# Sliding-window attention mixed with a long convolution: the spectrum's products reordered, lag 0 as a full tile, and a new order of all tasks

## The chip, the cores and the metric

The kernel runs on one core of a Trainium2 chip. Its time is the device time of one execution in microseconds (us); of several executions the median is given. The core has five queues of instructions that run beside each other: PE (matrix products; the weight loads of PE are shown apart as PEld), DVE and ACT (vector and scalar work), POOL, and SP, which here only starts transfers. Transfers (DMA) are started from the queues of SP, POOL and ACT and share 16 engines. Each queue runs its instructions strictly in the order in which they are given.

## What is computed

Two layers see the same input `x` (2048 positions, 640 channels) and are mixed by a gate per position. The first is an attention over 8 positions at distance 2, with 32 heads of 20 channels. The second is a state-space layer: a kernel `K` of 2048 lags for each channel is built from 192 complex modes, and the input is convolved with it by Fourier transforms.

```python
# attention
qkv = (x @ wqkv)                       # 32 heads of 20; keys and values at pos - 2*w, w = 0..7
o = softmax(q . k * scale) . v
a = o @ wo
# state-space layer
P = exp(logdA[:, :, None] * l)         # l = position, rounded to the input's type (bf16)
K = einsum("dn,dnl,dn->dl", Cc, P, dB).real
y = irfft(rfft(u, 2L) * rfft(K, 2L))[:L] + u * Dskip
# mix
g = sigmoid((x * gate_w).sum(-1))
out = g * a + (1 - g) * y
```

Since the position is rounded to bf16, many lags share one value: `K` takes only as many different values as there are rounded positions, and its spectrum is a product of those values with a constant matrix.

## The kernel before

The work is cut into some 1400 named tasks. Each task is a small piece of code for one engine: one group of matmuls, one eviction from PSUM, one transfer. The tasks' numbers stand in a list, `SEQ` (line 50), that was written out ahead of time; a letter behind a number picks the engine where there is a choice (A for ACT, D for DVE, S for SP, G for POOL). `Plan.emit` (line 132) issues the tasks in this order, so the list fixes the order of every queue. What a task needs, and which buffers it takes and gives back, decides only when it waits.

The stages, by the names of their tasks:

- `ld…` load the inputs; `turn` transposes `x` on PE and `late` makes queries, keys and values (L277), 60 groups of five products.
- The parameters of the modes are worked out on DVE and ACT and stored as bf16 pieces (`sp`). `kred` and `kmix` (L622 to L626) sum the modes for lag 0 and add `Dskip`.
- Attention goes in eight cores of 256 positions: `prod` (DVE, L335), `lg` (PE, L341), `max`, `exp`, `at`, then the values `vc` are loaded (L329), weighed by `pv` (DVE, L404), gathered on PE by `gat` (L410) and projected by `wo` (L428). The result goes to memory as `gaS`.
- The kernel's values are made in ten chunks: `arg` (PE, L758) makes the arguments, `act` (ACT, L770 and L772) takes sine and exponential, `pq` (DVE, L789 to L791) multiplies, `kmm` (PE, L807) sums over the modes, and `fin` (DVE, L865) stores 20 groups of 32 lags for every channel in `E`.
- The spectrum of the kernel has two parts, part 0 of six chunks (192 columns) and part 1 of four (128 columns). `move` puts the 640 lags of each part on 128 rows in `M5` = 5 tiles (`KE`). Then for each of 16 steps (8 blocks of four frequencies, real and imaginary part) a tile `W` of constants is loaded from memory (`wl`, L900, ring of three buffers) and `ks` (L912) multiplies it. Real parts have one more product at the end: lag 0, the same for all frequencies, from the single row `KD` against a row of ones (L916). `ske` evicts.
- The input's transform: `rows` load `x` in another layout (L993), `fu` (PE, L1027) and `fp` (PE, L1062) transform, `ta`, `tc`, `Y` (DVE, L1089 to L1095) multiply by the kernel's spectrum. `inv` (L1120) and `yp` (L1162) transform back; `psi` and `gaf` (L1136, L1142) load constants and the gated attention, and the result is scaled, added and stored (`tt`, `mx`, `st`, `out`).

Lag 0's value travels a way of its own: `kds` (L847) stores it, `kdl` (L851) loads it as one row, and `kdp` (L855) puts it in order on POOL.

Of the kernel before, what the change touches and what calls it, by code (L numbers as in the profile page):

```python
# [20 lines left out]
S = 2048  # L21
# [3 lines left out]
W = 8  # L25
# [25 lines left out]
13S 12S 24 18A 16S 23 35 36A 37A 20G 14S 15S 0G 4G 21 32 25 28 29 39 3S 22D 38 41 27 26 30 10S 8G 9S 100 11S 7S 108 5G 103G 17S 6S 2S 110 42 252S 109A 111A 31 104 105A  # L51
112 106 40 107A 43 44 113D 52 53 45 125 156 54 126D 157D 82 49 46 47 48 50 60D 61D 145 135 146A 136A 120 118 63 119A 149 133 114 150A 134A 55 115A 143 141 144A 142A 121D
62 57 51 68 69 70 77D 65 78 79 116 177 129 122 130A 83 178A 131 132A 71 185 186A 58 183 184A 147 66 148A 162 181 19G 1157G 56 72 101 1G 102G 1146G 163A 88A 182A 179 117A
180A 158 139 73 86 87 89 74 159A 137 140A 90A 138A 153 127 123A 76 85 93 128A 124 59 67 64 75 187S 84 91D 92 95 80 154A 260 97 98 262 94 96 81 99 550 253 261 160 166 161A
263 170 167A 171A 254 264 266 265 268 255 151 209 267 269 152A 256 211 257 210A 212A 270 271 272 296 33 298 34 176 155G 551 258S 552 164 554 217 553 555 556 273 274 558
557 559 560 561 562 564 563 565 297 566 299 165D 300 302 218D 568 567 569 570 571 572 573 547G 301 574 575 576 304 168 169D 578 577 579 174 175D 580 582 581 583 213 584
586 215 585 597 587 830 835 840 596 598 599 600 601 602 603 604 605 275 295S 259S 548G 588 214D 590 589 216D 276 277 606 591 607 608 592 610 303 198 609 612 278 611 613
614 616 615 617 593 618 620 619 621 594 622 305 624 623 625 279D 332 280 306 199A 172 626 628 281 283 173D 334 634 549 595 282D 643 636 627 629 630 632 631 633 642 644
645 646 647 648 649 307 1155S 650 652 651 653 219G 688 654 655 656 657 658 659 660 284 662 661 664 663 665 635 666 668 667 200 639 670 637 638 640 669 671 672 674 201D
285D 206 308 673 675 207A 680 309 676 677 641 310 689 286 678 287D 682 681 679 690 691 692 694 693 333 335 695 696 697 288 698 290 700 289A 699 701 336 338 337 702 683  # L60
703 704 705 684 188 706 707 339 685 340 291D 708 686 709 710 711 712 713 714 716 715 717 718 719 720 721 722 723 292 331G 311 312 734 735 687 726 313 728 724 727 736 189A
725 737 293A 241 738 740 341 342 243 739 741 242A 742 743 744 745 343 746 747 245 244D 316 246D 748 194 344 729 345 749 368 346 247 750 752 751 369 754 753 248D 756 195A
755 757 202 780 781 203A 370 372 731 371 758 760 759 761 196 762 208 249 294 347 348 373 764 374 376 197A 763 765 314 250A 766 730 768 375 377 317 767 769 315A 770 771
732 782 318A 783 319 220 378 251S 910 911 349 221A 784 320 786 379 785 787 321D 322 323A 733 772 774 788 380 324 326 789 325A 327A 381 773 790 792 791 793 204 777 404 794
775 776 796 190 191D 795 797 798 799 800 802 801 803 778 382 804 328 205A 806 805 807 329A 230 808 810 350 231A 809 811 405 812 813 814 815 816 817 912 913 351A 192 914
916 234 406 352 355 193A 915 917 918 919 235A 353 920 407 922 354A 921 923 238 924 818 820 779 408 409 410 412 239A 926 356 819 925 928 927 929 821 357A 403G 367G 383 956
384 957 330 930 411 932 931 933 413 823 414 934 936 822 935 937 358 360 938 415 940 359A 361A 939 416 226 227A 941 942 362 364 944 417 363A 365A 943 945 440 385 388 442
824 386 418 825 391 946 958 236 947 959 387A 960 441 443 962 389 237A 961 963 826 392 828 390A 827A 393A 829A 444 445 228 229A 446 448 948 447 224 964 966 449 232 225A
965 967 968 394 233A 450 419 366 1003 420 950 451 395A 396 970 452 969 397A 222 972 398 453 949 951 971 973 223A 952 974 976 400 975 399A 977 978 401A 439S 1002 240 1147S
1148S 1149S 1150G 1151G 1152S 1153S 1154G 402 421 424 454 455 476 422 979 980 982 423A 981 983 425 984 986 985 987 477 988 989 426A 831 478 479 990 992 833 832A 991 993  # L70
1004 834A 1005 953 427 954 1006 428 1008 1007 429A 1009 836 1010 430 837A 994 955 480 1012 1011 1013 431A 838 1014 995 1016 1015 839A 1017 432 1018 433A 1019 481 434 1020
# [611 lines left out]
class KGen:  # L683
# [51 lines left out]
    def plan(self, pl, pa, pk, hold, params, opened, fin):  # L735
# [4 lines left out]
        for c in range(NCH):  # L740
# [41 lines left out]
            for u in range(3):  # L782
# [543 lines left out]
```

## Time and profile before

| | |
|---|---|
| median of three runs | 404.74 us (402.11 to 405.25) |
| the profiled execution | 401.13 us, of which 399.3 us are the span of its instructions |
| mean granted clock of PE | 0.935 of full speed |
| busy | PE 333.3, DVE 300.0, ACT 302.3, POOL 50.9 us |
| moved by DMA | 49.86 MB, 125 GB/s over the span |

The profile gives for each instruction its engine, line, output and inputs, start and duration. Matmuls are pipelined: their durations overlap, so the pace of a block is read from the starts. In a timeline a row is a start, a duration, the engine and line, output and inputs, and how many instructions were merged; brackets hold the idle time of the engine before it and what ended that. "Issue" in brackets means that the engine waited for nothing that the profile shows. In a row of groups the two numbers behind the bar are the busy time in us and the mean of one in ns. A view of windows gives the busy time of each engine in stretches of the span.

### The profile page before, as it was taken

To read this page: it belongs to the slowest core of one execution; us is meant where nothing else is said; L and a number is where in the kernel's file an instruction comes from. 1 tells how busy PE (TensorE), PEld (TensorE's weight loads), DVE (VectorE), ACT (ScalarE), POOL (GpSimd) and SP (SyncE) were. 2 spreads that over 40 slices of the span, in tenths; PEclk is the share of its full clock that TensorE was granted. 3 is DMA by queue.
4 is the path that set the end of the run, shared out by engine and by line. 5 is a ranking of instruction groups with operands and counts; after the bars stand their busy time and mean duration, and the time that the engine had idled before them with its cause. 6 is when DMAs were issued, how large, how long until landed. Compare 5 with 4: busy or idle time off the path is not lost. (4 is left out here: it accounts for less than half of the span.)

```text
span 399.3 us, 14980 instructions
## 1 busy us (share of the span) xinstructions
PE 333.3 (83%) x6664; PEld 209.5 (52%) x6686; DVE 300.0 (75%) x420; ACT 302.3 (76%) x456; POOL 50.9 (13%) x82
## 2 busy tenths in 40 slices
PE   0499997968897999899957999999899994799860
PEld 0355452333354446445432656668777793688750
DVE  4979996686898989889894486869689752347782
ACT  3989986786999899989955888877587652365782
POOL 8710011200300010120201000000000231000022
PEclk9989998599899999999985999999999997699996
DMA  8971557851313127160599724461032859744027
GB/s 278 380 182 32 170 149 197 150 142 23 78 16 76 48 64 144 31 144 3 129 187 173 155 76 107 93 203 30 16 103 77 286 138 222 165 125 135 3 70 197
DMA packets 55761, 49.86 MB, mean 125 GB/s; under 512 B 33534, under 2 KB 46752, under 8 KB 55696
## 3 DMA queue, kind: packets, MB, share of 16 engines
q1 hardware_dynamic: 50896, 34.93, 36.0%
q0 software_dynamic: 4080, 13.64, 13.1%
q8 instruction: 52, 0.85, 0.9%
q10 hardware_dynamic: 720, 0.33, 0.3%
q14 instruction: 13, 0.11, 0.1%
HBM read 37.00 MB, written 11.89 MB: 122 GB/s over the span
## 5 line engine op out<-in xcount | busy, mean ns | idle before, releaser
L770 ACT ACTIVATE big<-ar 128x576 bf16<-128x576 int16 x120 | 72.5, 654 | 20.2 <-PE ar L758 18.6
L277 PE MATMUL tb<-bufA 128*128 128x512 bf16 x278 | 75.4, 400 | 6.1 <-DMA bufA<-in_A_wqkv_dram 2.6
L912 PE MATMUL tb<-KE,W 128*64 128x192 bf16 (+1 forms) x1280 | 62.3, 242 | 8.8 <-DMA W<-c_spec 8.6
L758 PE MATMUL ar<-Rarg,L 64*128 64x288 bf16 (+1 forms) x480 | 55.3, 283 | 12.7 <-ACT big L770 10.2
L912 PEld LDWEIGHTS <-W 128*64 128x64 bf16 x1280 | 47.5, 114 | 15.9 <-DMA W<-c_spec 9.3
L772 ACT ACTIVATE big<-ar 128x832 bf16<-128x832 f32 x60 | 49.8, 869 | 4.7 <-PE ar L758 3.7
L277 PEld LDWEIGHTS <-bufA 128*128 128x128 bf16 x300 | 32.7, 122 | 35.9 <-issue 12.6
L404 DVE TENSOR_TENSOR pv<-vc,asb 128x4096 bf16<-128x4096 bf16 (+1 forms) x24 | 46.0, 1931 | 6.2 <-PE tb L410 6.1
L758 PEld LDWEIGHTS <-L 64*128 64x128 bf16 x480 | 19.0, 95 | 52.3 <-issue 48.8
L457 ACT ACTIVATE bufA<-tb 128x384 bf16<-128x384 f32 (+1 forms) x36 | 18.9, 528 | 20.6 <-PE tb L912 11.7
L807 PE MATMUL kps<-tbx 128*32 128x20 bf16 (+1 forms) x2560 | 25.9, 175 | 9.7 <-issue 9.7
L807 PEld LDWEIGHTS <-tbx 128*32 128x32 bf16 (+1 forms) x2560 | 22.4, 92 | 15.2 <-issue 12.9
L457 ACT ACTIVATE tbx<-ar 128x512 bf16<-128x512 f32 (+1 forms) x31 | 20.4, 699 | 11.6 <-PE ar L1062 7.5
L1089 DVE TENSOR_TENSOR tbx<-tbx,bufA 128x768 bf16<-128x768 bf16 (+1 forms) x32 | 14.5, 487 | 19.1 <-ACT bufA L457 14.0
L335 DVE TENSOR_TENSOR prod<-qk 128x2048 bf16<-128x2048 bf16 x20 | 24.1, 1220 | 4.1 <-PE lg L341 2.2
L428 PE MATMUL tb<-wo_sb,oT 128*128 128x320 bf16 x160 | 26.9, 306 | 0.0
L335 DVE TENSOR_TENSOR prod<-uga 128x2048 bf16<-128x2048 bf16 x20 | 24.1, 1220 | 3.3 <-PE lg L341 3.1
L791 DVE TENSOR_TENSOR tbx<-big 128x1280 bf16<-128x1280 bf16 x30 | 24.6, 818 | 0.0
L457 ACT ACTIVATE big<-ar 128x1024 bf16<-128x1024 f32 x19 | 18.7, 1023 | 7.3 <-PE ar L1027 7.1
L410 PE MATMUL tb<-pv,ind 128*64 128x512 bf16 (+1 forms) x192 | 23.1, 365 | 0.0
L789 DVE TENSOR_TENSOR tbx<-big 128x1024 bf16<-128x1024 bf16 x30 | 20.5, 685 | 1.0 <-ACT big L770 0.5
L790 DVE TENSOR_TENSOR tbx<-big 128x1024 bf16<-128x1024 bf16 x30 | 20.5, 685 | 0.0
(168 smaller groups left out, 527.7 us busy)
## 6 DMA issues: line engine op xcount, KB each, us to landing
W<-c_spec SPq DMA_DIRECT2D x32, 320.0 KB, 3.2
Sprm<-pc SPq DMA_DIRECT2D x12, 240.0 KB, 2.9
L<-Sprm SPq DMA_DIRECT2D x80, 36.0 KB, 3.1
vc<-vS SPq DMA_DIRECT2D x8, 327.5 KB, 6.7
vc<-vS POOLq DMA_DIRECT2D x8, 327.5 KB, 5.7
gaS<-ga SPq DMA_DIRECT2D x8, 320.0 KB, 2.8
uga<-gaS POOLq DMA_DIRECT2D x8, 320.0 KB, 10.9
asb<-aS SPq DMA_DIRECT2D x16, 128.0 KB, 2.8
```

What stands on the lines that cost most here:

```text
L277: nc.tensor.matmul(ppf, self.wq[:, kt, which * D + e:(which + 1) * D:5], self.xT[:, c0 // 1024, kt, c0 % 1024:c0 % 1024 + SC], start=(kt = ...
L335: nc.vector.tensor_tensor(b[e][:], self.part(ch, 0)[:, e, o:o + C].unsqueeze(1).to_broadcast([128, W, C]), win(self.part(ch, 1)[:, e, :], ...
L404: nc.vector.tensor_tensor(b["pv", e][:, 0:2 * n], taps, aw, ALU.mult)
L410: nc.tensor.matmul(b["op", e][64 * a:64 * a + 64, 0:n, :], self.twin, b["pv", e][:, a:2 * n:2, w, :], start=(w == 0), stop=(w == HV - 1), ...
L428: nc.tensor.matmul(apf[:, :320], b["oT"][:, e, i * 128:(i + 1) * 128], wo_sb[:, e, hf * 320:(hf + 1) * 320], start=(e == 0), stop=(e == 4))
L457: nc.scalar.activation(o, i, ACT.Identity)
L758: nc.tensor.matmul(ar[:, g2, a0:a0 + ncol], L[rows, sb, gp, l0:l0 + 128], R[rows, c0:c0 + ncol], start=True, stop=True, tile_position=(64 ...
L770: nc.scalar.activation(dst[:, 2 * gp:2 * gp + 2, sub, :], ar[:].bitcast(I16)[:, :, 0:2 * SW:2], ACT.Sin, scale=SCL)
L772: nc.scalar.activation(dst[:, 2 * gp:2 * gp + 2].rearrange("p g s n -> p g (s n)"), ar[:, :, 0:2 * EW], ACT.Exp)
L791: nc.vector.tensor_tensor(qq[:, :, :, :], trg[:, :, KI:].rearrange("p a (v m) -> p a v m", v=2), exq[:, :, KI:].unsqueeze(2).to_broadcast( ...
L807: nc.tensor.matmul(kps[32 * g:32 * g + 32, h, NM * ql:NM * ql + NM], pt[rows, k, v, :], qq[rows, k, v, :], start=(g not in started), stop= ...
L912: nc.tensor.matmul(kp[64 * c:64 * c + 64, fl], w["t"][:, nf * h + fl, m, :], self.KE[p][:, m, c].rearrange("p x g -> p (x g)"), start=(m = ...
```

## The change

Four edits.

1. In `kmm`, `ks` and `yp` the loops are turned: the index over which is summed goes outside, and the outputs go inside, so that products that add to the same place are no longer neighbours. The `start` flag is now set once for each PSUM bank, at the first product that writes it.
2. Lag 0 becomes a sixth tile of 128 rows: `KD` has 128 rows, zero but for the first, `one` likewise, and its products come first (`m = -1`) in the same loop as the five others.
3. A new task `kdz` on POOL zeroes `KD` before the values are put in.
4. `SEQ` is another list: all tasks in a new order, with other engines for 83 of them.

```diff
@@ KGen.plan, kmm
-                    for ql in range(4 * j, 4 * j + 4) if u == 1 else range(8):
-                        for v in range(2):
+                    for v in range(2):
+                        for ql in range(4 * j, 4 * j + 4) if u == 1 else range(8):
...
@@ KSpec
-        self.one = keep.tile([1, 64], BF16, name="one")
-        self.nc.gpsimd.memset(self.one[:], 1.0)
+        self.one = keep.tile([128, 64], BF16, name="one")
+        self.nc.gpsimd.memset(self.one[:], 0.0)
+        self.nc.gpsimd.memset(self.one[0:1], 1.0)
...
-        self.KD = kk.tile([1, 2, 80, 4], BF16, name="KD")
+        self.KD = kk.tile([128, 2, 80, 4], BF16, name="KD")
...
-        t = pl.add("kdl", "SG", load, deps=[t], after=self.past)
-        self.kd = pl.add("kdp", "G", lambda _: nc.gpsimd.tensor_copy(self.KD[:].rearrange(...), ...), deps=[t])
+        t = pl.add("kdl", "SG", load, deps=[t] + self.past)
+        z = pl.add("kdz", "G", lambda _: (opened(), nc.gpsimd.memset(self.KD[:], 0.0)), deps=self.past)
+        self.kd = pl.add("kdp", "G", lambda _: nc.gpsimd.tensor_copy(self.KD[0:1].rearrange(...), ...), deps=[t, z])
...
@@ KSpec.part, spec
-                    for fl in range(nf):
-                        for m in range(M5):
+                    first = -1 if ro == 0 else 0
+                    for m in range(first, M5):
+                        for fl in range(nf):
                             for c in range(2):
-                                nc.tensor.matmul(kp[64 * c:64 * c + 64, fl], w["t"][:, nf * h + fl, m, :], self.KE[p][:, m, c]...,
-                                                 start=(m == 0), stop=(m == M5 - 1 and ro == 1), ..., tile_position=(0, 64 * c))
-                        if ro == 0:
-                            for c in range(2):
-                                nc.tensor.matmul(kp[64 * c:64 * c + 64, fl], self.one[:], self.KD[:, c, 8 * c0:8 * c1]...,
-                                                 start=False, stop=True, ..., tile_position=(0, 64 * c))
+                                wt = self.one[:] if m < 0 else w["t"][:, nf * h + fl, m, :]
+                                ke = self.KD[:, c, 8 * c0:8 * c1] if m < 0 else self.KE[p][:, m, c]
+                                nc.tensor.matmul(kp[64 * c:64 * c + 64, fl], wt, ke.rearrange("p x g -> p (x g)"),
+                                                 start=(m == first and fl == 0), stop=(m == M5 - 1), ..., tile_position=(0, 64 * c))
...
@@ Conv.tail, fin
-                for k, v in enumerate(vs):
-                    for ro in range(2):
+                for ro in range(2):
+                    for k, v in enumerate(vs):
...
-                                                 start=(ro == 0), stop=(ro == 1), ...)
+                                                 start=(ro == 0 and k == 0), stop=(ro == 1), ...)
```

The new list in the places that the prediction reads. On DVE, `kred` and `kmix` now come before the products of core 0 (before: between those of core 1). On PE the end of part 0 of the spectrum reads

```
before  ... ks0,12 fp06 ks0,13 fu15 ks0,13 ks0,14 fp07 ks0,14 ks0,15 fu16 fu17 ks0,15 fu18 fu19 ks1,0 ks1,1 fp10 ks1,2 ...
after   ... ks0,9 fp05 fu17 ks0,9 fu18 fu19 ks0,10 (2) move (2) ks0,11 (2) fp06 (2) ks0,12 (2) fp07 ks0,13 (2) ks0,14 (2) ks0,15 (2) ks1,0 fp07 fp10 ks1,1 ...
```

On POOL the queue reads `rows0` to `rows7`, then the values of cores 5 and 6, `phi1`, the values of core 7, `psi`, `gaf`; before, five of the rows and the values of cores 5 and 7 were SP's. At the start the first two loads of `x` and one of the weights have moved to ACT's queue.

More of the change, by code (lines that the diff above doesn't have):

```diff
@@ L900, in load @@
                 queue(nc, e).dma_start(w["t"][:].rearrange("p f m x -> p (f m x)"), self.w_d[k])
-            ld = self.ld = pl.add(f"wl{p}{k}", "S", load, after=[getattr(self, "ld", None)] + self.past, acq=["W"])
+            ld = self.ld = pl.add(f"wl{p}{k}", "S", load, deps=self.past, after=[getattr(self, "ld", None)], acq=["W"])
             for h in range(4 // nf):
@@ L1162, in fin @@
                                 nc.tensor.matmul(yp[64 * j:64 * j + 64, h, 160 * k:160 * k + 160], psi[64 * h:64 * h + 64, 32 * j + v, ro, :], C[64 * h:64 * h + 64, 64 * ro + 32 * j + v, :],
-                                                 start=(ro == 0), stop=(ro == 1), skip_group_check=True, tile_position=(64 * h, 64 * j))
+                                                 start=(ro == 0 and k == 0), stop=(ro == 1), skip_group_check=True, tile_position=(64 * h, 64 * j))
             def scale(_, n=n, vs=vs):
```

82 lines of the change are left out of this document (40 added, 42 removed).

## The prediction

> **What bounds the kernel now.** I read the totals first, then the busy time by stage, because an average over 399 us hides which engine sets which stretch.
>
> ```profile
> span 399.3 us, 14980 instructions
> PE 333.3 (83%) x6664; PEld 209.5 (52%) x6686; DVE 300.0 (75%) x420; ACT 302.3 (76%) x456; POOL 50.9 (13%) x82
> ```
>
> ```profile
> 68.00:205.00 137.00, 122.83 (x2523) 60.45 (x2538) 116.97 (x146) 122.72 (x189) 14.70 (x22) 0.94 0.41 87
> 205.00:212.00 7.00, 0.52 (x54) 0.41 (x43) 5.63 (x8) 0.23 (x1) 0.00 (x0) 0.69 1.30 179
> 212.00:220.00 8.00, 7.68 (x63) 2.83 (x51) 3.17 (x4) 5.69 (x11) 1.43 (x2) 0.63 1.06 175
> 220.00:330.00 110.00, 107.92 (x2442) 79.67 (x2438) 81.98 (x121) 83.86 (x129) 7.25 (x12) 1.00 0.43 117
> 330.00:350.00 20.00, 12.28 (x244) 10.38 (x242) 6.67 (x17) 6.38 (x12) 0.66 (x2) 0.68 0.90 198
> 350.00:376.00 26.00, 24.39 (x660) 20.25 (x657) 16.85 (x39) 16.28 (x23) 0.00 (x0) 0.98 0.32 93
> ```
>
> The columns are window, length, then busy time of PE, weight loads, DVE, ACT, POOL, the granted clock, the DMA share and GB/s. From 68 to 205 us three engines share the work: PE 90%, ACT 90%, DVE 85% busy, and PE is without work for 14.2 us. From 220 to 330 us PE is busy 98% while DVE and ACT are at 75 and 76%: this stretch, and again 350 to 376 us (94%), is set by PE alone. Two holes interrupt it, 205 to 212 and 330 to 350 us; in both the DMA share is high (1.30, 0.90) and the clock falls (0.69 and 0.63 around the first, 0.68 in the second). All of the spectrum's products (L912, L916) lie after 219.6 us, that is, where PE is the bound.
>
> **Lag 0, the largest term.** The real half of each frequency block ends with a product of one row; the imaginary half has none. The PE timeline shows both, first with 192 columns (part 0), then with 128 (part 1):
>
> ```profile
> 219.60 0.60 PE L912 MATMUL tb<-KE,W 128*64 128x192 bf16 x10
> 220.13 0.27 PE L916 MATMUL tb<-KD,one 1*64 1x192 bf16 x2
> ...
> 221.07 0.40 PE L341 MATMUL lg<-prod,ind 128*32 128x512 bf16 x4
> ```
>
> ```profile
> 227.22 1.02 PE L912 MATMUL tb<-KE,W 128*64 128x192 bf16 x20
> 228.17 0.30 PE L758 MATMUL ar<-Rarg,L 64*128 64x288 bf16 x2
> ```
>
> ```profile
> 357.26 1.28 PE L912 MATMUL tb<-KE,W 128*64 128x128 bf16 x40
> 358.38 0.61 PE L1062 MATMUL ar<-big,L 128*64 128x128 bf16 x16
> 358.83 0.45 PE L912 MATMUL tb<-KE,W 128*64 128x128 bf16 x10
> ...
> 361.09 1.07 PE L1120 MATMUL ar<-GAB,bufA 64*128 64x128 bf16 x32
> ```
>
> Read starts against starts, since the durations overlap; the two lines left out are a second block of ten and its lag 0. Part 0: with lag 0 a task takes 221.07 - 219.60 = 1.47 us, without it 228.17 - 227.22 = 0.95 us. The two products of one row are not the cost; 0.95 us buys ten pairs, 0.095 us a pair with the entry included. Lag 0 waits for the array to empty and the next tile waits again, 0.26 us for each frequency. As a sixth tile of the same shape it costs a pair: the next frequency's. Taken at 0.095 us, a task of 12 pairs takes 0.95 + 2 x 0.095 = 1.14 us and saves 0.33 us. Part 1: 361.09 - 358.83 = 2.26 us with, 358.38 - 357.26 = 1.12 us for 20 pairs without, so 24 pairs take 1.34 us, and 0.92 us are saved. The number of tasks follows from the rows
>
> ```profile
> L916 PE MATMUL tb<-KD,one 1*64 1x192 bf16 x64 | 8.6, 265 | 0.0
> L916 PE MATMUL tb<-KD,one 1*64 1x128 bf16 x64 | 7.8, 240 | 0.0
> ```
>
> as 64 / 4 = 16 and 64 / 8 = 8. Together 16 x 0.33 + 8 x 0.92 = **12.6 us** of PE. What of it shortens the run: two of the 24 tasks, of part 1, run within the hole at 330 to 350 us, where transfers set the pace, which takes off about 2 us; the rest lies in stretches where PE is busy 94 to 98%. I take 10.5; the upper bound is 12.6. The lower one supposes that the shortened stretch couples to the other engines as 68 to 205 us does: DVE and ACT rise to some 82% of it, and if PE then idled 10% of the 125 us outside the hole, 12.5 us where it idles 3.7 now, 2 would remain.
>
> Weighed against this is a rule that would undo it. The Trainium skill, "TensorE: Matmul & The Clock Gate", Part 3 (what overlaps and what doesn't), lets a weight load run beside a matmul only in another row group. By it the new 128-row loads would stand exposed; that outcome is the fourth rival below. The 20 matmuls of 0.95 us above bring 20 weight loads with them and speak against it, as does the other branch that the same page gives, the background weight buffer.
>
> **The other loop orders.** In the kernel matmuls (L807) and the last transform (L1162) the products that add to the same place move apart.
>
> ```profile
> 84.39 0.65 PE L807 MATMUL kps<-tbx 128*32 128x20 bf16 x64
> 381.76 1.85 PE L1162 MATMUL cy<-C,psi 64*64 64x160 bf16 x96 [1.28 <-DVE C L459]
> ```
>
> 64 products in 0.65 us are 10 ns each, 96 in 1.85 us 19 ns each; and L912 adds five times in a row to one place at the same pace as it changes place. Nothing waits for an addition, so I take 0 for the new loop orders, with 1 us either way. The zeroing of KD is one more POOL instruction, scaled from
>
> ```profile
> L696 POOL MEMSET L<- 128x1536 bf16 x2 | 2.8, 1392 | 0.0
> ```
>
> to 640/1536 of 1.39 = 0.58 us, on an engine busy 13% and 150 us ahead of the first use. Nil; without that cover it would cost its 0.58 us.
>
> **The new order of tasks.** I read the list as five queues, one for each engine, with the numbers above 549 one higher than before. Four moves touch something that the trace shows.
>
> (a) The sum and mix that make lag 0's value (kred, kmix) come ahead of the attention's first products on DVE. Now they are what the first sine waits for:
>
> ```profile
> 62.45 1.15 DVE L622 TENSOR_REDUCE k<-wr 128x5 f32<-128x960 f32 x1
> 65.15 1.28 ACT L770 ACT_TABLE_LOAD   x1 [2.69 <-DVE kdb L626]
> 67.14 0.30 PE L758 MATMUL ar<-Rarg,L 64*128 64x288 bf16 x2 [2.45 <-ACT big L770]
> ```
>
> ACT loses 2.7 us, PE 2.5. The same 1.15 us on DVE are now spent earlier, where DVE is busy too. Gain 1.5 (0 to 2.7).
>
> (b) The last first-transforms (fu18, fu19) come while six W tiles' spectrum tasks of part 0 remain, not none. That moves the eight gathers of gaS (gaf), which wait for fu19, under other work. Now:
>
> ```profile
> 325.44 5.22 POOL L1142 DMA_DIRECT2D uga<-gaS  x8 [12.96 <-PE ar L1027]
> 337.81 2.34 PE L912 MATMUL tb<-KE,W 128*64 128x128 bf16 x40 [5.64 <-DMA W<-c_spec]
> ...
> 345.44 2.35 PE L912 MATMUL tb<-KE,W 128*64 128x128 bf16 x40 [1.86 <-DMA W<-c_spec]
> ```
>
> While the gathers run (325 to 345 us) two W tiles more arrive in 345.44 - 337.81 = 7.6 us, one in 3.8, and part 1 uses one in 1.12 to 2.26. The waits shown are 7.5 us; the two blocks of 40 take 2.34 us where the one at 357.26 took 1.28, and with the transforms between them I put the slow clock at 3 us more: 10.5 in all. In the new order the gathers meet W tiles of part 0, which last 2 x 1.14 = 2.3 us each, with three transforms and two moves between: the six tiles last some 16 of the 20 us, and the ring of three holds two or three of them when the gathers begin. Four more in 16 us is just the supply, so I leave half of the 10.5 and take a gain of 5. Bounds: 3 us worse than now (six tiles at 3.8 us are 23 us, three past the 20), and all of the 10.5.
>
> (c) All eight row loads for the first transform go to POOL's queue, ahead of the values of cores 5 to 7; five went to SP's.
>
> ```profile
> 196.05 2.35 POOL L993 DMA_DIRECT2D uga<-in_A_x_dram  x3 [23.71 <-issue]
> 200.40 12.56 SPq L993 DMA_DIRECT2D uga<-in_A_x_dram  x5
> 211.82 0.26 PE L807 MATMUL kps<-tbx 64*32 64x20 bf16 x13 [6.48 <-issue]
> ```
>
> While they run PE stops for 6.5 us inside a block of L807 with nothing that it waits for, at a DMA share of 1.30, and runs at 0.63 for the next 8 us, worth 3: 9.5. I read it as PE's own instructions arriving late through the same engines. The new order has the chunk-6 products at the same place behind the loads, so I expect the hole again: 0, with 9.5 either way. The queue behind them is safe if the loads overlap (third rival). The Trainium skill, "Runtime: NRT & Kernel Launch", Instruction fetch mechanics, calls the crossing into a new block mostly hidden; by it this term is a gain of 9.5, and the row says that here it was not hidden.
>
> (d) The first two x loads move to ACT's queue behind the exponential of log_dt:
>
> ```profile
> 3.77 0.21 ACT L557 ACTIVATE dtb<-ldt 128x5 bf16<-128x5 bf16 x1 [1.28 <-DMA ldt<-in_B_log_dt_dram]
> 12.23 1.89 PE L184 MATMUL ar<-ident,uga 128*128 128x128 bf16 x16 [6.18 <-DMA uga<-in_A_x_dram]
> ```
>
> They are issued past 4 us. PE starts at 12.2 us on them; I take a loss of 1 (0 to 3). The projections wait for all weights anyway. For the rest of the order, where every engine keeps its work, I take 0; half of PE's 14.2 idle us between 68 and 205 is the bound on each side, 7.
>
> **The sum.** 10.5 + 1.5 + 5 - 1 = 16 us. The profiled execution took 401.13 us, of which 399.3 are span; 401.1 - 16 = 385.1. The median of the runs is 404.74, 3.6 above the profiled one, and runs are what is measured: **388.7 us**. The terms' bounds combined as independent reach 13 us on the fast side and 17 on the slow one (lag 0 and the two collisions make most of it); eight in ten I put at 14 either way.
>
> **Rivals.** Their prices need two more views, the DMA issues (size, median us to landing) and the group of weight loads:
>
> ```profile
> vc<-vS POOLq DMA_DIRECT2D x8, 327.5 KB, 5.7
> ...
> uga<-in_A_x_dram POOLq DMA_DIRECT2D x3, 320.0 KB, 7.6
> ```
>
> ```profile
> L912 PEld LDWEIGHTS <-W 128*64 128x64 bf16 x1280 | 47.5, 114 | 15.9 <-DMA W<-c_spec 9.3 <-issue 1.8
> ```
>
> First, the gain sticks in new waits: lag 0 brings only 5, about midway between its lower bound and the forecast's value, and the collision of (b) costs what it does now, because fewer PE microseconds per W tile make each tile more urgent. 5 + 1.5 - 1 = 5.5, so 395.6 profiled and 399 by the runs. For it: in the 20 us of gathers the transfers set the pace whatever PE does. Against: DVE and ACT are at a third there, and the new order brings PE other work at that place.
>
> Second, better than forecast: the hole of (c) closes as well, because SP's queue carries no rows any more. 16 + 9.5 = 25.5, 379 by the runs. Against: the same bytes move in the same time.
>
> Third, slower: the row loads on one queue run one after the other. The three on POOL take 7.6 us each to land; eight in series are 61 us, and the values of core 5 stand behind them with 5.7 more. In the new DVE queue some 45 instructions lie between the product that frees the rows' space and the first use of those values, 42 us by the row of 68 to 205 (146 in 137 us), so serial loads would stall DVE, and all behind it, about 25 us: 401.1 + 25 - 12 + 3.6 = 418. It decides from 36 us for the eight. For it: all software descriptors come from one engine. Against: eight gathers on the same queue were issued in 5.2 us and done within 20.
>
> Fourth, the change doesn't do what it says: the loads of the sixth tile are exposed, 128 x 0.11 us (the weight load's row) = 14 us, which eats the 12.6 and, with the small terms, leaves no change: 404.
>
> **How the numbers follow.** The forecast has 0.50, the first rival 0.20, the second 0.13, the third 0.12, the fourth 0.05. About 1% (4 us) is what a measurement of this kernel can tell from no change. The forecast and the second rival are beyond it, of the first about a third (0.07) is not: faster 0.50 + 0.13 + 0.13 = 0.76, same 0.07 + 0.05 = 0.12, slower 0.12. The range 375 to 403 leaves out the third and fourth rivals and little else; the forecast's own is 382 to 396.
>
> **What would show it.** Right: no product of one row; a real half of part 0 in about 1.14 us and of part 1 in 1.34; PE's busy time near 320; the first sine about 2.5 us sooner after the first softmax; fewer and shorter waits of the spectrum for W, none of 5 us. Wrong: the pairs of a real half stretching beyond 0.1 us; a wait of DVE for values between cores 4 and 5; a hole at the gathers as long as now; or PE idle spread through the spectrum stretch while DVE and ACT are near 90%.

## The result, and the profile after

The changed kernel takes 384.65 us (median of 4 runs, 382.61 to 386.59), the kernel before, measured beside it, 403.43 us (4 runs, 400.72 to 405.25): a ratio of 0.954, interval 0.946 to 0.962. The forecast was 388.7 us, its own range 382 to 396. The profiled execution of the changed kernel took 386.59 us, of which 384.8 are span, so the two profiles lie 14.5 us apart in span where the medians lie 18.8 apart. For e1 to e4 below I compare medians: three of the 13 executions of the kernel before that were measured beside them were shorter than the rest (394.69 to 398.96 us at a granted clock of 0.942 to 0.957, the others 400.86 to 404.41 at 0.923 to 0.939), and by the ratios built on these three (1.000, 0.986, 0.974, 0.979) each of the four would be unclear.

The totals of the page after:

```profile
span 384.8 us, 14995 instructions
PE 314.6 (82%) x6666; PEld 209.9 (55%) x6686; DVE 304.5 (79%) x429; ACT 293.2 (76%) x445; POOL 59.3 (15%) x95
```

PE's busy time is 18.7 us shorter, with the same matmuls but for two records. The windows by stage (window, length, PE, weight loads, DVE, ACT, POOL, granted clock, DMA share, GB/s) show that both holes of before are still there, at 200 to 210 and at 305 to 330 us:

```profile
200.00:210.00 10.00, 4.49 (x159) 2.36 (x148) 3.58 (x5) 3.56 (x8) 0.00 (x0) 0.68 1.05 189
...
305.00:330.00 25.00, 17.67 (x422) 16.37 (x418) 13.75 (x27) 8.78 (x16) 5.20 (x8) 0.93 0.89 203
```

A ledger by milestones tells where the time went. From the timelines of before, ACT and then PE, the first sine and the end of the spectrum (371.46 + 1.31 = 372.77 us; its first product at 219.60 stands in the prediction):

```profile
66.44 1.74 ACT L770 ACTIVATE big<-ar 128x576 bf16<-128x576 int16 x3
...
371.46 1.31 PE L912 MATMUL tb<-KE,W 128*64 128x128 bf16 x40
```

The same points after, with the end of the softmax ahead of the first sine:

```profile
66.40 0.60 ACT L368 ACTIVATE at<-lg 128x512 bf16<-128x512 f32 x1 [0.27 <-PE lg L364]
...
68.31 2.28 ACT L771 ACTIVATE big<-ar 128x576 bf16<-128x576 int16 x4
...
213.68 0.36 PE L918 MATMUL tb<-KD,one 128*64 128x192 bf16 x4
213.87 0.99 PE L918 MATMUL tb<-KE,W 128*64 128x192 bf16 x20
214.79 0.42 PE L759 MATMUL ar<-Rarg,L 64*128 64x288 bf16 x4
...
349.23 0.41 PE L918 MATMUL tb<-KD,one 128*64 128x128 bf16 x8
349.47 1.28 PE L918 MATMUL tb<-KE,W 128*64 128x128 bf16 x40
350.59 0.61 PE L1064 MATMUL ar<-big,L 128*64 128x128 bf16 x16
...
353.63 2.60 PE L918 MATMUL tb<-KE,W 128*64 128x128 bf16 x80
```

| stretch | before, us | after, us | difference | forecast |
|---|---|---|---|---|
| start to first sine | 66.44 | 68.31 | +1.9 | -0.5 (a, d) |
| first sine to first spectrum product | 153.16 | 145.37 | -7.8 | 0 (c, rest of the order) |
| spectrum, first product to last | 153.17 | 142.55 | -10.6 | -15.5 (lag 0, b) |
| from there to the end of the span | 26.5 | 28.6 | +2.0 | 0 |

The sum, -14.5, is near the forecast's -16, but each of its parts misses, by 2.0 to 7.8 us. The first row is within the spread of single profiles: in the seven kernels of this document with the new order and this start (the changed one, e1, e3, e4, e5, e7 and e8) the first sine begins at 66.3 to 68.5 us. Only lag 0's price can be read directly: a real half of part 0 now takes 214.79 - 213.68 = 1.11 us, one of part 1 350.59 - 349.23 = 1.36 us.

### The profile page after: what moved, and what is told of

The parts are those of the page before. It is cut to its first block, busy times and chain, and to the rows that moved or that the text cites. A ratio compares the mean times of both kernels' runs of the same rounds, so it can differ in the third digit from the quotient of the medians.

```text
span 384.8 us, 14995 instructions
## 1 busy us (share of the span) xinstructions
PE 314.6 (82%) x6666; PEld 209.9 (55%) x6686; DVE 304.5 (79%) x429; ACT 293.2 (76%) x445; POOL 59.3 (15%) x95
## 5 line engine op out<-in xcount | busy, mean ns | idle before, releaser
L771 ACT ACTIVATE big<-ar 128x576 bf16<-128x576 int16 x120 | 71.1, 657 | 12.7 <-PE ar L759 12.3
L278 PE MATMUL tb<-bufA 128*128 128x512 bf16 x280 | 74.0, 396 | 4.7 <-issue 1.3
L759 PE MATMUL ar<-Rarg,L 64*128 64x288 bf16 (+1 forms) x480 | 51.0, 280 | 16.3 <-issue 8.8
L918 PE MATMUL tb<-KE,W 128*64 128x192 bf16 (+1 forms) x1280 | 53.5, 236 | 9.6 <-DMA W<-c_spec 7.3
L458 ACT ACTIVATE bufA<-tb 128x384 bf16<-128x384 f32 (+1 forms) x31 | 16.8, 541 | 20.0 <-PE tb L918 19.8
L429 PE MATMUL tb<-wo_sb,oT 128*128 128x320 bf16 x160 | 28.5, 322 | 2.7 <-ACT ga L438 2.7
L808 PEld LDWEIGHTS <-tbx 128*32 128x32 bf16 (+1 forms) x2560 | 22.8, 92 | 10.5 <-issue 8.4
L438 ACT ACTIVATE ga<-tb,g_sb 128x320 bf16<-128x320 f32 x27 | 14.4, 537 | 13.5 <-PE tb L429 9.2
L330 POOL DMA_DIRECT2D vc<-vS x14 | 10.1, 737 | 93.7 <-DVE pv L405 91.7
L185 PE MATMUL ar<-ident,uga 128*128 128x128 bf16 x80 | 7.9, 264 | 17.4 <-DMA ident<-c_ident 16.9
L429 PEld LDWEIGHTS <-oT 128*128 128x128 bf16 x160 | 14.8, 103 | 11.9 <-issue 4.7
## 6 DMA issues: line engine op xcount, KB each, us to landing
uga<-gaS POOLq DMA_DIRECT2D x8, 320.0 KB, 10.2
```

Source lines behind the costliest of these rows:

```text
L278: nc.tensor.matmul(ppf, self.wq[:, kt, which * D + e:(which + 1) * D:5], self.xT[:, c0 // 1024, kt, c0 % 1024:c0 % 1024 + SC], start=(kt = ...
L429: nc.tensor.matmul(apf[:, :320], b["oT"][:, e, i * 128:(i + 1) * 128], wo_sb[:, e, hf * 320:(hf + 1) * 320], start=(e == 0), stop=(e == 4))
L458: nc.scalar.activation(o, i, ACT.Identity)
L759: nc.tensor.matmul(ar[:, g2, a0:a0 + ncol], L[rows, sb, gp, l0:l0 + 128], R[rows, c0:c0 + ncol], start=True, stop=True, tile_position=(64 ...
L771: nc.scalar.activation(dst[:, 2 * gp:2 * gp + 2, sub, :], ar[:].bitcast(I16)[:, :, 0:2 * SW:2], ACT.Sin, scale=SCL)
L808: nc.tensor.matmul(kps[32 * g:32 * g + 32, h, NM * ql:NM * ql + NM], pt[rows, k, v, :], qq[rows, k, v, :], start=(g not in started), stop= ...
```

## Experiments: which part of the change brought what

**e1** has the new order but the loops and the one-row lag 0 of before; **e2** has the old order with the new loops and the sixth tile; **e3** differs from e1 in one operand pair:

```
e1 -> e3   for fl: for m: ... ; if ro == 0: for c:
-   nc.tensor.matmul(kp[..., fl], self.one[0:1], self.KD[0:1, c, 8 * c0:8 * c1]..., start=False, stop=True, ...)
+   nc.tensor.matmul(kp[..., fl], self.one[:],   self.KD[:, c, 8 * c0:8 * c1]...,   start=False, stop=True, ...)
```

**e4** is the changed kernel with that pair cut to one row (`self.one[0:1]`, `self.KD[0:1, ...]`) at its new place, ahead of the tiles and for all frequencies of a task together.

> The new order of tasks with the old loops and the old lag 0 (one row, behind each frequency). Theory A (lag 0's emptying of the array is worth about 11 us, the new order some 7 us on its own): 395 to 397 us by the runs, PE's busy time near 333, real halves of part 0 at 1.47 us. Rival B (the gain is the order's alone): 385 to 387. Rival C (all is lag 0 and the loops): 402 to 404.

> The old order of tasks with the new loops and lag 0 as a sixth tile of 128 rows; KD is zeroed in the task that fills it. Theory A: 391 to 394 us by the runs, the hole at the row loads as before, the hole at the gathers as long or longer. Rival B: 402 to 404. Rival C: 385 to 387.

> As the changed kernel, with the old loops in all three places and lag 0 as a 128-row product behind the five tiles of each frequency. Theory A (the turned loops are worth nothing): 383 to 387 us by the runs, real halves of part 0 at 1.1 us. Rival D (products that add to one place one after the other wait): 390 or more, and the halves longer.

> As the changed kernel, but lag 0's product has one row again; it stands first, for all frequencies of the task together. Theory A (the cost is for each change of shape, not for each product): one change in a task instead of two or four, so about 24 x 0.2 = 5 us of PE more than the changed kernel, 387 to 390 us by the runs, real halves of part 0 at 1.3 and of part 1 at 1.5 us. Rival E (each product of one row costs its 0.26 us wherever it stands): 12 us more, 396.

Measured, medians, on one chip with a kernel before of 402.58 us: e1 396.9 us (394.73 to 400.84, 10 runs), e2 389.66 (388.7 to 394.06, 4), e3 385.85 (384.98 to 386.8, 4), e4 387.21 (386.38 to 390.12, 4). These are the times expected by the theory A of e1, e3 and e4; e2 is 1.3 us below its own, so that by the medians the edit is worth 12.9 us in the old order.

From e1 to e3, by one operand pair alone, the time falls by 11.0 us, and the longest run of e3 is 7.9 us below the shortest of e1. The PE timeline of a real half of part 0 in e1:

```profile
211.74 0.60 PE L915 MATMUL tb<-KE,W 128*64 128x192 bf16 x10
212.27 0.27 PE L919 MATMUL tb<-KD,one 1*64 1x192 bf16 x2
212.47 0.60 PE L915 MATMUL tb<-KE,W 128*64 128x192 bf16 x10
213.00 0.27 PE L919 MATMUL tb<-KD,one 1*64 1x192 bf16 x2
213.20 0.42 PE L759 MATMUL ar<-Rarg,L 64*128 64x288 bf16 x4
```

and in e3:

```profile
213.56 0.60 PE L915 MATMUL tb<-KE,W 128*64 128x192 bf16 x10
214.00 0.25 PE L919 MATMUL tb<-KD,one 128*64 128x192 bf16 x2
214.08 0.58 PE L915 MATMUL tb<-KE,W 128*64 128x192 bf16 x10
214.50 0.25 PE L919 MATMUL tb<-KD,one 128*64 128x192 bf16 x2
214.68 0.42 PE L759 MATMUL ar<-Rarg,L 64*128 64x288 bf16 x4
```

Start against start, 1.46 us against 1.12: the same two products for each frequency, of the same 192 columns, cost no more than their neighbours, 0.09 us a pair, once they have their shape. In e3 lag 0 stands where it always stood, behind each frequency, so it is the shape that counts and not the place. e4 says the rest. Its real half of part 0 keeps the one row, but gathered:

```profile
212.79 0.35 PE L918 MATMUL tb<-KD,one 1*64 1x192 bf16 x4
213.07 1.02 PE L918 MATMUL tb<-KE,W 128*64 128x192 bf16 x20
214.02 0.42 PE L759 MATMUL ar<-Rarg,L 64*128 64x288 bf16 x4
```

It takes 214.02 - 212.79 = 1.23 us, and one of part 1 takes 1.48: in both parts 0.12 us more than with the full tile, though a task of part 1 has twice as many frequencies. So the change of shape is paid once for a task instead of once for each frequency; e4's median lies only 1.4 us above e3's, with overlapping runs. e3, with all old loops, and the changed kernel (384.65, measured apart) are too close to tell apart: turning the loops gave nothing that these runs can show.

The order: from the kernel before to e1 5.7 us by the medians, with overlapping runs, and from e2 to e3 3.8 (e3 has the old loops beside the new order), where the runs do not overlap. The milestones of the ledger place both parts. From the first sine to the first spectrum product the two kernels with the old order take 153.2 (before) and 154.1 us (e2), those with the new one 145.5 (e1), 147.1 (e3) and 145.4 (the changed kernel). From there to the last spectrum product the two without the sixth tile take 153.2 (before) and 153.6 us (e1), those with it 139.5 (e2), 142.1 (e3) and 142.6. So the order's gain lies ahead of the spectrum, and lag 0's in it. In the waits of PE over the whole run, before had these rows (what was waited for, us, times, longest):

```profile
PE ar L758 <- ACT big L770: 10.2, 24, 2.4
...
PE tb L912 <- DMA W<-c_spec: 8.6, 4, 5.6
```

e2, with the old order, still has the first (9.8 us, 23 times); e1, with nothing but the new order, has

```profile
PE tb L915 <- DMA W<-c_spec: 4.7, 2, 3.2
PE ar L759 <- ACT big L771: 3.9, 14, 0.6
```

and the changed kernel has the same row for the sines, and for W

```profile
PE tb L918 <- DMA W<-c_spec: 7.3, 4, 4.0
```

PE waits 6.3 us less for the sines that free the buffers of its argument products (2.45 us of the 10.2 are the wait for the first sine itself): PE's other work is better placed between them. But that is not the 7.8 us of the ledger. Over that stretch, before and in the changed kernel (columns as above), the windows are

```profile
66.44:219.60 153.16, 131.48 (x2607) 63.80 (x2623) 125.87 (x157) 129.79 (x201) 16.13 (x24) 0.91 0.49 98
68.31:213.68 145.37, 125.96 (x2662) 63.30 (x2675) 122.95 (x157) 126.33 (x200) 19.68 (x31) 0.93 0.49 104
```

PE's idle time falls only from 21.7 to 19.4 us. Of the 6.3 us, 1.75 lay ahead of the first sine, and 2.4 come back: 0.6 as waits for the exponentials, 0.6 as one for a load, 1.2 as stalls without a visible wait (8.7 to 9.9 us in those of 0.5 us and more), among them a new one of 3.25 us that ends at 110.92 us. Over the whole run these stalls add up to 9.7 us before, 13.4 in e1 and 13.7 in the changed kernel. The other 5.5 us are busy time. The argument products now stand in longer rows, and all 480 of them take 51.0 us after 55.3; 16 products of `gat` and five of `wo` are no longer in the stretch, while twelve argument products and 64 of `kmm` are new in it; and the granted clock is 0.93 after 0.91. How much each of these brings, no run separates.

The W row tells of (b): the order alone brings the waits from 8.6 to 4.7, and the faster lag 0 puts them back, to 7.1 in e3, which differs from e1 in that operand pair alone, and 7.3 in the changed kernel. In the old order it leaves them as they are (8.4 in e2). Nor do fewer waits for W make e1's spectrum any shorter: in their place stand 4.3 us of stalls without a visible wait, after 1.0 before, and a wait of 1.5 us for ACT.

## Experiments: the three collisions that stayed

The changed kernel's start, hole and gathers, from three timelines (ACT's queue and PE; POOL and PE; POOL and PE):

```profile
6.04 1.01 ACTq L167 DMA_DIRECT2D uga<-in_A_x_dram  x2
7.09 0.54 ACTq L242 DMA_DIRECT2D ident<-c_ident  x1
...
16.92 1.86 PE L185 MATMUL ar<-ident,uga 128*128 128x128 bf16 x16 [16.92 <-DMA ident<-c_ident]
```

```profile
190.21 6.24 POOL L995 DMA_DIRECT2D uga<-in_A_x_dram  x8 [14.38 <-DVE prod L336]
...
206.31 0.42 PE L759 MATMUL ar<-Rarg,L 64*128 64x288 bf16 x2 [5.51 <-issue]
```

```profile
305.00 5.20 POOL L1144 DMA_DIRECT2D uga<-gaS  x8 [7.83 <-PE ar L1029]
...
315.86 3.10 PE L918 MATMUL tb<-KE,W 128*64 128x192 bf16 x40 [4.03 <-DMA W<-c_spec]
```

Four kernels move one of these each, and nothing else in the list of tasks (a letter is the queue: G is POOL's, S SP's, A ACT's):

```
e5  - 1361G ... 1368G (gaf, behind psi3)          + 1361S ... 1368S behind 1144 (the last W load)
e6  - 3A 4A 0A (ldx0, ldx1, identity)             + 0G 4G behind 18G (log dt), 3S behind 12S
e7  - 1152G 1153G 1154G 1155G (rows4 to rows7)    + 1152S 1153S behind 456 (asb5), 1154S 1155S behind 402 (gaS3)
e8  - 1148G ... 1155G (all rows)                  + 1148S ... 1155S behind 456 (asb5)
```

> The changed kernel (384.65 us, profiled 386.59) with the eight loads of the attention's output for the mix (gaf, 2.6 MB) taken from POOL, where they go out at 305 to 310 us and meet the first six W loads of part 1, and put on SP's queue behind the last W load (issued at about 350 us). Theory: the waits on W (7.3 us behind 4 halves) and the slow granted clock behind them come from this collision; they fall to under 2 us, the spectrum stage ends 5 to 8 us sooner, and the loads land by 364 us, before the first mix at 367: 377 to 381 us. Rival: the first W loads of part 1 wait for their own reasons (their buffers come free late, psi's loads), the waits stay over 5 us: 384 to 387. Second rival: the loads land after the first mix, and the tail gives the gain back: no W wait, but 383 to 388.

> The changed kernel with the issue of the identity matrix and the first two pieces of x (ldid, ldx0, ldx1) taken from ACT, where they stand behind the activation dtx and go out at 7.1 us, and put on SP (ldx0, behind the first four small loads) and POOL (identity, ldx1, behind the log dt load). Theory: the late start (first transposition ended at 14.7 instead of 12.2 us, the kernel's PE starting for good at 16.9) came from that position; the start comes 2 to 4 us sooner, and half to all of it reaches the end: 381 to 384. Rival: at the start all loads share a saturated DMA, another load is late in its place, the first sine keeps its 68 us: 384 to 387.

> The changed kernel with four of the eight row loads of x for the transform (rows4 to rows7) taken from POOL, which issues all eight at 190 to 196 us, and put on SP: two behind asb5 (215 us), two behind gaS3 (220 us); all are needed at 245 us. Theory: PE's hole of 5.5 us at 201 to 206 us, in which DVE, ACT and POOL stand too, comes from the DMA engines being full with row loads (share 1.03 to 1.07 from 195 to 210): it shrinks to under 2 us, and the clock in 205 to 210 rises from 0.50: 379 to 382 us. Rival: the hole moves to the place of the later loads (215 to 230 us), with the same length: 384 to 387.

> The changed kernel with all eight row loads on SP behind asb5 (out from 215 us), so that none is under way from 195 to 210 us. Theory: the hole at 201 to 206 us goes altogether; but the loads keep the DMA engines full from 215 to about 230 us, and the hole of 5 to 6 us comes back there, or W's loads 3 to 5 are late by as much: 383 to 388 us. Rival: the hole has nothing to do with the row loads: it stays at 201 to 206, 384 to 388. Second rival: only the loads that POOL issues (software descriptors) make it; SP's do not, and no hole over 2 us is left: 378 to 382.

Measured, each of 4 runs, beside a kernel before of 402.21 us: e5 381.38 us (ratio 0.944, 0.936 to 0.952), e6 383.0 (0.952, 0.947 to 0.957), e7 383.72 (0.953, 0.948 to 0.958), e8 382.89 (0.950, 0.943 to 0.958). Against the changed kernel's 384.65 each alone is a gain of 0.9 to 3.3 us, which the overlapping intervals of the ratios do not establish; the traces say more.

**e5.** The waits on W are gone, one of 0.62 us is left, and the spectrum ends at 348.75 instead of 356.23 us: the gathers were what W's tiles collided with. But the timeline of PE in the last transform shows a new stall:

```profile
352.25 1.85 PE L1122 MATMUL cy<-GAB,bufA 64*128 64x128 bf16 x60 [1.21 <-ACT C L458]
357.22 3.58 PE L1122 MATMUL cy<-GAB,bufA 64*128 64x128 bf16 x68 [3.11 <-issue]
```

It stands inside a block of one instruction form, PE waits for nothing that the profile shows, and the DMA engines are full (columns as above):

```profile
354.00:356.00 2.00, 0.10 (x4) 0.00 (x0) 1.34 (x2) 0.43 (x1) 0.00 (x0) 1.00 1.24 186
```

The stall came along with the gathers, so 7.5 us at the spectrum's end became 4.0 at the end of the last products, between the first theory and the second rival.

**e6.** The first matmul starts at 12.33 instead of 16.92 us and waits for x, not for the identity. The first sine moves from 68.31 to 63.95, the spectrum's end by 2.8 us, the median by 1.7. The theory holds; of the 4.4 us at the first sine more than half reaches the spectrum's end. The first sine of the changed kernel is a late one among its like, though: the five kernels with the moved start (e6 and e9 to e12) have it at 63.95 to 64.66 us, the seven without at 66.3 to 68.5, a difference of 2.9 us by their medians.

**e7 and e8.** In e8 no row load is under way at 200 us, and PE's wait there is 1.38 us, which the profile puts down to a sine (the last section has more on it). The stall stands where the loads went (PE's timeline):

```profile
200.82 0.30 PE L759 MATMUL ar<-Rarg,L 64*128 64x288 bf16 x2 [1.38 <-ACT big L771]
...
218.91 2.68 PE L918 MATMUL tb<-KE,W 128*64 128x192 bf16 x34 [2.83 <-issue]
```

So the rows make the hole, and SP's loads make it too (the second rival is out), but shorter than the 5 to 6 us of the theory. e7, with half of the rows left on POOL, has stalls of 1.89 us at 201, 1.19 at 219 and 0.81 at 224 in place of 5.51 and 1.59: the stall under 2 us that its theory asks for, but not the 379 to 382 us.

**Together.** e10 adds e5, e6 and e8. e9 spreads instead: one or two rows at a time between SP's other tasks from 190 to 229 us, and one gather behind every second W load of part 1. e11 takes e9's rows and e5's gathers; e12 is e11 with three of the gathers ahead of the last three W loads.

```
e9   + 1148S behind 366, 1149S behind 455, 1150S behind L90, 1151S behind L91, 1152S behind 456, 1153S 1154S behind 402, 1155S behind 856
     + 1361S ... 1367S behind the W loads 3, 5, 7, 9, 11, 13, 15 of part 1, 1368S behind 1367S; start as e6
e11  rows and start as e9; gaf as e5
e12  as e11, but 1361S, 1362S, 1363S behind the W loads 12, 13, 14
```

> The three moves of e5, e6 and e8 together in the changed kernel: gaf behind the last W load on SP; identity, ldx0 and ldx1 ahead at the start; all eight row loads on SP behind asb5. If the three cost separate things, their gains add: from the changed kernel's profiled span of 384.8 us the runs took 5.1 (e5), 3.9 (e6) and 4.5 (e8), less the spread of one profile, so 371 to 375 us. Rival: each gain is given back elsewhere, since a stage that ends sooner only meets the next full DMA sooner (e5 already showed 3.1 us of stall in the last transform): 376 to 380.

> As e10, but no group of loads goes out in one piece: the eight row loads stand one or two at a time between SP's other tasks (behind gaS2, ast5, L90, L91, asb5, twice behind gaS3, behind wl05: about 193 to 235 us), and the gaf loads one behind every second W load of part 1, the last two behind the last. Theory: what stops PE is a stretch in which the DMA engines are over 1.0 busy, not the place of it; spread, neither the hole near 201 or 217 nor the 3.1 us stall in the last transform of e5 comes back, and W waits stay under 2 us: 367 to 372 us, 2 to 5 below e10. Rival: every such load slows the one beside it, the loads of W, L and asb on the same queue are late instead: as e10 or up to 4 above it, 372 to 378.

> Start as e6, row loads spread as in e9, gaf in one piece behind the last W load as in e5 and e10. In e9 the spread rows brought the transform's end to 295.6 us (e10: 301.2), but the gaf loads between the W loads cost 8 stalls of PE, 8.0 us, and the spectrum stage took 51.8 us from there (e10: 43.1). With the better half of each: spectrum stage ends at about 339, and the rest takes the 28.8 us of e10: 366 to 369 us, 5 to 8 below e10's fast runs of 374 to 375. Rival: e9's early transform end was an accident of its one profile or of POOL's and SP's queues there, and is not repeated: 372 to 376.

> As e11, with the first three gaf loads one behind each of the W loads 12, 13 and 14 of part 1, and five behind the last. Theory: half of the full-DMA stretch falls into the end of the spectrum stage, where each load costs PE up to 1 us (e9: 8.0 us for eight), and the stall behind it (e5: 3.1 us, e10: two of about 2) shortens by as much: within 1.5 us of e11. Rival: the stall is not in proportion to the loads in one piece but needs a stretch longer than some us, and five loads make none: 2 to 4 us below e11.

Measured: e10 377.68 us (374.23 to 381.63, 4 runs) and e9 375.84 (373.44 to 381.03, 4 runs; ratio 0.930, 0.924 to 0.937) beside a kernel before of 402.98; **e11 372.91** (370.84 to 379.74, 5 runs; ratio 0.928, 0.921 to 0.935) and e12 377.99 (376.09 to 381.8, 5 runs; ratio 0.940, 0.934 to 0.945) beside 402.21.

The gains seem to add, but e10 does not settle it: the medians of e5, e6 and e8 lie 3.3, 1.7 and 1.8 us under the changed kernel, 6.8 together, and e10's lies 7.0 under it, which is inside its rival's 376 to 380 us; of its four runs two took 374.23 and 375.02, about as its theory says, and two 380.34 and 381.63. e9's 375.84 is in its rival's range, too. By their single profiles, spreading helps the rows: in e9, e11 and e12 the transform ends at 295.6, 296.9 and 298.8 us, in e10 at 301.2. It does not help the gathers. In e9 PE's waits have

```profile
PE tb L918 <- issue: 8.0, 8, 3.0
```

against 4.1 us in three waits in e11. Not all eight are the gathers', as the expectations of e11 and e12 have it: two, 2.3 us, stand at 214 to 220 us, where the rows are. Five, 5.6 us, stand beside the gathers between 325 and 347 us; e11 has one of 1.9 us there and one of 2.8 in the last transform. From the transform's end to the end of the span e9 takes 78.4 us and e11 73.1, so e9's theory is wrong for the gathers. In time e9 and e11 are not told apart: their ratios' intervals overlap. e11 ends its spectrum at 340.6 us (expected 339) and needs 29.3 us from there (expected 28.8). Its 371.7 us profiled lies above the 366 to 369 expected mainly because I left out the 1.8 us between span and time. Its median lies in its rival's 372 to 376, but the rival's reason does not hold, as the early end of the transform is there again. e11 is faster than both kernels: its ratio's interval ends at 0.935, where the changed kernel's begins at 0.946. e12 fits neither of its theories: its one profile, of its longest run, is already 4.4 us later than e11's at the first product of the last transform (319.9 against 315.5 us), before the first gather is issued. Why its median is 5 us above e11's stays open.

## Why the prediction was right or wrong

**Lag 0: right in mechanism and size.** Forecast 1.14 and 1.34 us for the real halves, measured 1.11 and 1.36; forecast 10.5 us on the path, measured 11.0 from e1 to e3. PE's busy time, forecast near 320 us for 12.6 less, is 314.6; the edit alone, in e2, brings it to 320.8, 12.5 less than before. What is shown is that the change of shape costs the time; that the array empties meanwhile is my reading, and no run shows it. The fourth rival is out: 128-row loads of the sixth tile are not exposed, as a real half with 24 pairs takes 1.36 us against about 1.12 for 20 pairs.

**Loop orders: right**, as far as e3 can tell.

**(a) Right, then used up.** Between the end of the first softmax and the first sine lay 66.44 - 62.46 = 3.98 us before and lie 68.31 - 67.00 = 1.31 now: the 2.69 us of waiting for kred and kmix are gone. But the softmax itself comes 4.5 us later. Most of that is (d): the seven kernels with this start end the first softmax at 64.6 to 67.0 us, the five with e6's at 62.3 to 63.1. Not all of it need be, as e2 with the old start has 64.5, in one profile.

**(d) Mis-sized.** I counted the two x loads behind the exponential and missed the third load behind them, the identity, without which no transposition starts: the first transposition starts 4.7 us later (16.92 after 12.23), where I took 1. Of this the x loads make 2.5, as PE loads the first of `x` as weights at 14.73 us, and the identity the rest. e6 brings 4.4 back at the first sine and 2.8 at the spectrum's end, just inside the bound of 3.

**(b) Wrong in net.** I took 5 us; W's waits fell by 1.3. The reading that the new place has more PE work to cover the gathers was right by the order alone (8.6 to 4.7 us in e1). Two things failed. Fewer waits for W are not a shorter spectrum: e1's takes 153.6 us after 153.2, because other stalls took their place. And the term is not independent of lag 0: each W tile is used up faster, and 2.4 to 2.6 us of waiting come back in the new order. This is the first rival's mechanism at a smaller size; it did not eat lag 0's gain.

**(c) Right:** 5.51 us of hole after 6.48, at the same stage, and no DVE wait for values, so the third rival is out; the second, that the hole closes, too. The reason given is supported by e8, where the hole left with the loads, and by e5, where a new one came with the gathers. The Trainium skill, "Runtime: NRT & Kernel Launch", Instruction fetch mechanics, which I weighed there, calls the crossing into a new block mostly hidden. That holds for most blocks and not for all: five of the changed kernel's 52 instruction transfers go with a stall of PE of 0.5 us or more, 13.7 us together, and at a DMA share above 1 such stalls were 5.5 us long, 2.8 in e8 and 3.1 in e5. The last section shows that the instructions are what was late.

**The rest of the order: the step that failed.** I took 0 +- 7 and the middle gained 7.8. A row that could have told me a part was in the trace: besides the first sine PE waits 23 times, 7.8 us, for a sine to free its buffer. I looked at which tasks change engine and place, not at what the new list puts between the argument products. Nor did I see that the list would add 3.9 us of stalls without a visible wait. The rest of the gain is busy time, and its causes are not separated.

**From profile to runs.** The profiled time was forecast as 385.1 and is 386.59; the 3.6 us that I added for the runs had the wrong sign, since this time the profiled execution was the longest of four, 1.9 above the median. The forecast's miss of 4.0 us is that correction (5.5) less 1.5 by which the terms missed in sum. That this is only 1.5 is luck: the middle's 7.8 us, which no term had, made up for 2.4, 4.9 and 2.0 at the start, in the spectrum and at the end.

## What to carry to other kernels

A tiny product among large ones costs the change of shape and not its rows; pad it to its neighbours' shape with zeros when the memory is there. When a schedule is judged by its list, look at the longest repeated wait in the trace and at what the list puts into it, before looking at single moves. Where large groups of loads fill the DMA engines, look for stalls of PE without a visible wait and for the instruction transfers in them; here, spreading the row loads brought the transform's end 2 to 6 us forward against one group of eight, by single profiles. And two terms that draw on the same resource (fewer PE microseconds per tile, fewer waits for tiles) are not to be added as if independent.

## What the hardware showed that I had not expected

PE's instructions can be seen arriving. The page of the profile has a queue of the kind "instruction", 52 transfers and 0.85 MB, which is about 64 bytes for each of PE's 6666 + 6686 matmuls and weight loads, and 16 KB or 256 such instructions for each transfer:

```profile
q8 instruction: 52, 0.85, 0.9%
```

The view of the DMA queues, cut to the 2 us of the hole in the changed kernel from 203 to 205, and to the 1 us from 354 to 355 in e5's last stall, shows one transfer each:

```profile
q8 instruction: 1, 0.02, 4.5%
```

```profile
q8 instruction: 1, 0.02, 9.0%
```

By the trace's packets, the first began at 203.32 us and took 1.44, and PE, idle from 200.80, went on at 206.31; the second began at 354.44 and took 1.44, and PE, idle from 354.10, went on at 357.22. The longest stall of before (transfer from 208.98 to 210.39, PE on at 211.82) and that of e8's rows (215.94 to 217.26, on at 218.91) are alike. In all 20 stalls of 0.5 us and more in these four runs PE goes on 1.2 to 1.7 us after the end of such a transfer.

The stalls also stand at fixed places. Three of the five that e9 has beside the gathers are

```profile
335.08 0.75 PE L918 MATMUL tb<-KE,W 128*64 128x128 bf16 x19 [0.78 <-issue]
339.63 0.97 PE L918 MATMUL tb<-KE,W 128*64 128x128 bf16 x27 [0.51 <-issue]
...
346.65 0.75 PE L918 MATMUL tb<-KE,W 128*64 128x128 bf16 x19 [2.98 <-issue]
```

Counted along PE's matmuls and weight loads, the five come behind the instructions 11426, 11682, 11938, 12194 and 12450, each 256 after the last. The hole of the changed kernel at 201 us comes behind 5797 and its next stall, 1.59 us, behind 6565, three times 256 on; e8, with the rows later, has its 2.83 us behind 6565, and behind 5797 the 1.38 us put down to a sine, which end 1.45 us after an instruction transfer, too. So a stall without a visible wait is here a late block of 256 instructions, and it stands where the block before it ends.

How late it is depends on more than full engines. PE goes through small products fast:

```profile
271.37 1.43 PE L808 MATMUL kps<-tbx 64*32 64x20 bf16 x152
274.97 0.46 PE L808 MATMUL kps<-tbx 128*32 128x20 bf16 x40 [2.18 <-issue]
```

The 256 instructions ahead of this stall of the changed kernel took 1.28 us, and it stands 2.18 us with the DMA share at 0.00; the transfer had begun 0.75 us after the block's first instruction. Ahead of the hole at 201 us they took 1.40 us, and the transfer began 3.92 us after the first. So some 1.4 to 2 of the 5.5 us, as an estimate from e8's 1.38 and this 2.18, would stand there without the row loads. And full engines need not bring a stall. In the changed kernel, with psi and W under way at 372 GB/s,

```profile
300.00:305.00 5.00, 5.00 (x108) 5.00 (x104) 3.51 (x6) 2.41 (x5) 0.00 (x0) 1.00 1.00 372
```

PE is busy throughout (a transfer of instructions began at 300.86), where at a like share of 1.03 but 183 GB/s, with the row loads in pieces of 160 bf16 elements by the code, it stands:

```profile
200.00:205.00 5.00, 0.80 (x71) 0.59 (x61) 1.95 (x3) 1.25 (x3) 0.00 (x0) 0.86 1.03 183
```

Two cases do not make a rule of the piece size; no run changed it alone. The other surprise is the identity, 32 KB, issued at 7.09 us behind the large loads of the start and landed only at 16.92.
